# Filler matmuls of the identity in the opening, activation-table loads issued on their own, and a last sum taken bank by bank, in a windowed attention with a feed-forward layer

## The chip, the cores and the metric

The kernel runs on one core of a Trainium2 chip. The metric is the device time of one execution in microseconds (us). Before the change it is 925.33 us, the median of three runs (924.84 to 925.38).

The core has five engines with queues of their own, each strictly in the order of the program: TensorE (PE; its weight loads are shown as PEld), VectorE (DVE), ScalarE (ACT), GpSimd (POOL) and SyncE (SP), which here only issues DMAs. An instruction that waits for a semaphore holds up everything behind it on its engine.

## The reference, cut to what matters

```python
q, k, v = ...                      # 8 batches x 8 heads x 576 positions x 64, float32
scores = q @ k.T / sqrt(64)        # causal, window of 64 positions, rest masked
attn   = softmax(scores); o = attn @ v
x = o.transpose(0, 2, 1, 3).reshape(4608, 512)
h = x @ w_in                       # 512 -> 2048, weights are float64
g = h * tanh(softplus(h))          # "mish"
out = g @ w_out                    # 2048 -> 512, float32
```

## The kernel before, in words

The 4608 tokens are cut into 12 chunks of 384. The 512 channels are four pairs of heads; a *unit* is one pair of one chunk, so there are 48 units. For a unit, PE makes the scores (24 small matmuls, L322), DVE adds the mask and takes the row minimum (L343), ACT takes the exponential (L347), DVE divides by the sum (L353, L354, L356), the result is turned (in chunks 0 to 2 by PE, L377, with a copy by ACT or DVE, L382; later by a DVE transpose and 12 small DMAs, L394 and L400), and PE multiplies with v (L413). ACT and DVE split the result into a rounded part `xh` (L426) and a rest `xl` (L427).

The feed-forward layer walks over 16 slices `f` of the 2048 inner columns. `ffn_in` makes `h` for one chunk and slice with 12 matmuls of 384 columns (L439: four channel blocks, each as three products of high and low parts); `activate` applies mish on ACT (L468); `halves` splits it into two parts (`g`, on ACT and DVE in chunks 0 and 1, L476 and L477, on POOL later, L480 and L482); `ffn_out` adds 9 matmuls of 512 columns (L502) into three banks of PSUM, one for each 128 tokens: `acc0` to `acc2` (list `A`) for every chunk but chunk 1, which uses `at0` to `at2` (list `B`). After slice 15, DVE copies banks 0 and 2 and ACT bank 1 into SBUF (L515), and SP stores each (L517). The two banks `h0` and `h1` (list `H`) hold `h` in turn; only 384 of their 512 columns are used.

The weights come as 64-bit floats, one slice after the other (`st`, 1 MB each, L238), and `weights` rebuilds them as two rounded 32-bit parts: an absolute value (on ACT for slices 0 to 6, L247; on DVE afterwards, L250), four further passes on DVE (L252, L253, L255, L260), a cast on ACT (L267) and a subtraction on DVE (L270). The load of slice f waits until the L260 pass of slice f-2 is done (`pace`). This work, and the attention of chunks 0 and 1, fill the opening.

Nothing is issued in the order in which the Python code names it. Every piece of work is a `Task` with an engine, a cost from the table `COST`, a rank, and the tasks that it depends on. `Plan.order` plays the program through with these costs, engine by engine, takes at each point the ready task of the lowest rank, and the tasks are then emitted by their planned start. So a changed cost or rule moves instructions on all engines. From chunk 2 on, the PE tasks are chained in a fixed order and only the other engines are planned. ACT needs one table of functions for the exponential (and the absolute value) and another one for mish; before the change the table load is put in by the build in front of the first activation that needs it.

Of the kernel before, what the change touches and what calls it, by code (L numbers as in the profile page):

```python
# [16 lines left out]
P = 128  # L17
# [8 lines left out]
    "h": 2.08, "hcc": 0.52, "acc": 2.06, "acc1": 0.687, "scores": 0.95, "values": 0.95, "tr": 0.65,  # L26
    "ttr": 0.21, "small": 0.19, "norm3": 0.46, "norm6": 0.87, "xl": 0.47, "pT": 0.45, "turn": 0.97,
    "exp": 0.385, "xh": 0.42, "mish": 0.40, "gh": 0.46, "gl": 0.47, "poolgh": 0.51, "poolgl": 1.01,
    "abs": 1.06, "absv": 0.62, "ts": 0.62, "stt": 1.14, "wh": 0.96, "store": 0.65, "issue": 0.45, "move": 0.62,
}  # L30
LATENCY = {"PE": 0.30, "DVE": 0.16, "ACT": 0.22, "POOL": 0.16}
SELF = {"PE": 0.0, "DVE": 0.11, "ACT": 0.10, "POOL": 0.10}
TABLE_LOAD = 1.3
SLOW_UNTIL, SLOW = 70.0, 1.2
LANDING = 1.9
BYTES_PER_US = 330e3
# [19 lines left out]
class Task:  # L56
    def __init__(self, n, engine, cost, emit, rank, table, size):
        self.n, self.engine, self.cost, self.emit, self.rank = n, engine, cost, emit, rank
        self.table, self.size = table, size
        self.name = f"{cost} {rank:g}"  # L60
        self.deps, self.users = set(), []
        self.start = self.done = None


class Plan:
# [6 lines left out]
    def add(self, engine, cost, emit, reads=(), writes=(), rank=0.0, after=(), table=None, size=0, chain=False):  # L72
        t = Task(len(self.tasks), engine, COST.get(cost, cost), emit, rank, table, size)
        t.deps.update(after)
        for b in reads:
            b.read(t)
        for b in writes:
            b.write(t)
        t.deps.discard(t)
        if chain:  # L80
            if self.last_pe:
                t.deps.add(self.last_pe)
            self.last_pe = t
        self.tasks.append(t)
        return t

    def order(self):
        left = {}
        ready = {e: [] for e in ("PE", "DVE", "ACT", "POOL", "SP")}
        free = dict.fromkeys(ready, 0.0)  # L90
        free.update(SP=0.7, ACT=2.5, POOL=4.0)
        table, moving = "exp", 0.0
        for t in self.tasks:
            left[t] = len(t.deps)
            for d in t.deps:
                d.users.append(t)

        def release(t):
            return max([d.done if d.engine != t.engine or d.engine == "SP" else d.start + d.cost + SELF[d.engine]
                        for d in t.deps], default=0.0)  # L100

        for t in self.tasks:
            if not left[t]:
                ready[t.engine].append((release(t), t))
        for _ in self.tasks:
            at, e = min((max(free[e], min(r for r, _ in ready[e])), e) for e in ready if ready[e])

            def key(rt):
                r, t = rt
                switch = t.table not in (None, table)  # L110
                return t.rank + SWITCH * switch, t.n

            now = [rt for rt in ready[e] if rt[0] <= at + 1e-6]
            pick = min(now, key=key)
            ready[e].remove(pick)
            t = pick[1]
            t.start = at
            if e == "ACT" and t.table not in (None, table):
                table = t.table
                t.start += TABLE_LOAD  # L120
            free[e] = t.start + t.cost * (SLOW if e == "PE" and at < SLOW_UNTIL else 1.0)
            if e == "SP":
                moving = max(moving, t.start + LANDING) + t.size / BYTES_PER_US
                t.done = moving
            else:
                t.done = free[e] + LATENCY[e]
            for u in t.users:
                left[u] -= 1
                if not left[u]:
                    ready[u.engine].append((release(u), u))  # L130
        return sorted(self.tasks, key=lambda t: (t.start, t.n))
# [6 lines left out]
def tile_window_attn_mish_ffn(  # L138
# [229 lines left out]
    def turn_pe(u, rank, engines, chain):  # L368
        pr, prb = u.pr
        pr = pr.rearrange("p (j k) -> p j k", k=P)  # L370
        pT, pTb = u.pT = pT_ring.take()
        for h in range(2):
            t_ps, tb = u.t[h]

            def tr(h=h, t_ps=t_ps):
                for m in range(NM):
                    nc.tensor.transpose(t_ps[:, m * P:(m + 1) * P], pr[:, h * NM + m, :], ident)  # L377

            add("PE", "tr", tr, reads=[prb], writes=[tb], after=[u.normed[h]], rank=rank, chain=chain)

            def copy(h=h, t_ps=t_ps):
                (nc.scalar.copy if engines[h] == "ACT" else nc.vector.tensor_copy)(  # L382
                    pT[:, :, h * NM:(h + 1) * NM, :].rearrange("p r m i -> p m r i"),
                    t_ps[:, :CH].rearrange("p (m r i) -> p m r i", m=NM, i=32))
# [109 lines left out]
    def ffn_out(c, f, rank, chain):  # L494
        acc = B if c == 1 else A
        g, gb = pend.pop((c, f))

        def emit(banks):
            for t in banks:
                ts_ = slice(t * P, (t + 1) * P)  # L500
                for i, (a, part) in enumerate(((0, 0), (0, 1), (1, 0))):
                    nc.tensor.matmul(acc[t][0], g[:, a, ts_], ws[f][:, 1, part, :],  # L502
                                     start=f == 0 and i == 0, stop=f == NF - 1 and i == 2)

        parts = [[t] for t in range(NTT)] if f in (0, NF - 1) else [range(NTT)]
        for part in parts:
            sums[c] = add("PE", "acc" if len(part) > 1 else "acc1", lambda part=part: emit(part), reads=[gb, wbufs[f]],
                          writes=[acc[t][1] for t in part], rank=rank, chain=chain, after=[sums[c]] if c in sums else [])
        outs.append((c, f))
        pump()  # L510
        if f == NF - 1:
            for t in range(NTT):
                o, ob = o_ring.take()
                eng = "DVE" if t % 2 == 0 else "ACT"
                add(eng, "store", lambda t=t, o=o: (nc.vector.tensor_copy if t % 2 == 0 else nc.scalar.copy)(o, acc[t][0]),  # L515
                    reads=[acc[t][1]], writes=[ob], rank=-1)
                add("SP", "issue", lambda t=t, o=o: nc.sync.dma_start(out[c * CH + t * P:c * CH + (t + 1) * P, :], o),  # L517
                    reads=[ob], rank=10 ** 6, size=P * DO * 4)

    units = []  # L520
    for c in range(NCHUNK):
# [39 lines left out]
    def bank(pool):  # L561
        rot[0] += 1
        return pool[(rot[0] - 1) % 3]

    def tail(i):
        u, r = units[i], RANK_U[i]
        if i >= 4:
            pool = B if i < 8 else A
            u.t = [bank(pool), bank(pool)]
            u.o = bank(pool)  # L570
        turn_pe(u, r, ("ACT", "ACT") if 4 <= i < 8 else ("ACT", "DVE"), False)
        values(u, r, False)
        refill_v(i)
        x_parts(u, r)
# [32 lines left out]
    def late(c, f):  # L607
        ffn_out(c, f, r_ffn(c, f) + 15, False)
        if (c, f) == (0, NF - 1):
            for i in range(8, 12):  # L610
                front(i)
                if i > 8:
                    tail(i - 1)
            tail(11)
# [27 lines left out]
    for i in range(4 * NPAIR, len(units)):  # L642
        g = first + (i - 4 * NPAIR) // 2 * 2
        run(g - 2 if i >= 4 * NPAIR + 2 else (5, 6)[i % 2], "s", i)
        run(g, "v", i)
    pr_ring.extend([wa_ring.tiles[1].bitcast(F32)[:, :HM * P]], wa_ring.bufs[1:])
    step, held = 0, []
    for g, steps in enumerate(groups):
        r = 1000 + 10 * step
# [20 lines left out]
        for c, f in held:  # L670
            ffn_out(c, f, r + 15, True)
        held = steps
    for c, f in held:
        ffn_out(c, f, 10 ** 5, True)

    tasks = plan.order()
    if REPORT:
        REPORT(tasks)
    for t in tasks:
        t.emit()  # L680


# [36 lines left out]
```

## Time and profile before

| | |
|---|---|
| median of three runs | 925.33 us (924.84 to 925.38) |
| profiled execution, its own time | 925.7 us |
| its span, first to last instruction | 923.8 us |
| PE busy | 900.7 us (97%) |
| DVE, ACT, POOL busy | 315.6, 364.2, 261.3 us |
| mean granted TensorE clock | 0.993 |
| ACT table loads | 64 |

One execution is taken apart. The page of the profile gives the busy time of each engine, the groups of instructions and the chain of work that ended last. The other views are cut by time: the chain in order of time, the timeline of single instructions, the waits (who stood idle until whom), and the stretches (busy time, granted clock and DMA traffic between two points). Times in them are from the start of the span. The granted clock is 1.00 at full speed; where the clock has no record yet, at the very start, it also reads 1.00.

### The profile page before, as it was taken

What the parts mean: (1) busy time and instruction counts of PE and PEld (TensorE: products, weight loads), DVE (VectorE), ACT (ScalarE), POOL (GpSimd) and SP (SyncE); (2) the same over time, 40 slices, a digit from 0 to 9 for tenths busy, and PEclk for the clock granted to TensorE, in tenths of its full rate; (3) what the DMA queues carried; (4) which work ended last, traced back from release to release, by engine and by line L of the source; (5) the groups of instructions that cost most, each with busy time, mean ns of one, the idle gap of its engine ahead of it and who ended that gap; (6) DMA issues with size and microseconds to landing.
All of it is one profiled execution on the core that took longest, in us unless ns stands there. A gap on an engine that the chain in (4) does not pass through costs nothing.

```text
span 923.8 us, 17003 instructions
## 1 busy us (share of the span) xinstructions
PE 900.7 (97%) x6408; PEld 805.6 (87%) x6408; DVE 315.6 (34%) x969; ACT 364.2 (39%) x963; POOL 261.3 (28%) x337
## 2 busy tenths in 40 slices
PE   5779999999999999999999999999999999999998
PEld 4569998888898998899899989988998899899896
DVE  6979973442314404304124034042141240400000
ACT  6875436964634414315225134243242341411110
POOL 1000000023233323433343244233333532432432
PEclk9989999999999999999999999999999999999999
DMA  8754412222324203302312222132122220100000
GB/s 271 234 194 153 167 69 72 73 93 74 100 61 128 83 20 94 111 26 89 115 27 83 67 81 78 56 93 77 60 87 66 79 81 23 54 37 1 35 1 35
DMA packets 79763, 77.28 MB, mean 84 GB/s; under 512 B 10049, under 2 KB 73025, under 8 KB 77633
## 3 DMA queue, kind: packets, MB, share of 16 engines
q1 hardware_dynamic: 79536, 75.96, 26.0%
q8 instruction: 51, 0.84, 0.4%
q14 instruction: 32, 0.25, 0.1%
q10 hardware_dynamic: 144, 0.23, 0.1%
HBM read 56.10 MB, written 9.44 MB: 71 GB/s over the span
## 4 chain that ended last, share of the span: by engine, by line
PE 92%; DVE 4%; ACT 2%; DMA 1%; issue 0%; SPq 0%; ACTq 0%; DVEq 0%
PE h L439 43%; PE acc L502 38%; PE at L502 3%; PE at L322 3%; PE at L413 2%; PE h L413 1%; DVE pr L343 1%; DMA st<-w 1%; DVE pr L356 1%; DMA k_t<-kT 1%; PE acc L322 1%; DVE wa L255 1%; DVE wa L260 0%; ACT L468 0%; PE h L322 0%; PE acc L413 0%
## 5 line engine op out<-in xcount | busy, mean ns | idle before, releaser
L439 PE MATMUL h<-xh,w 128*128 128x384 f32 x1536 | 407.6, 338 | 3.4 <-ACT t L468 2.2
L439 PEld LDWEIGHTS h<-xh,w 128*128 128x128 f32 x1536 | 280.5, 189 | 10.6 <-ACT t L468 6.4
L502 PE MATMUL acc<-w,g 128*128 128x512 f32 x1224 | 288.0, 390 | 0.0
L502 PEld LDWEIGHTS acc<-w,g 128*128 128x128 f32 x1224 | 229.2, 188 | 48.0 <-POOL gx L482 0.3
L439 PE MATMUL h<-xl,w 128*128 128x384 f32 x768 | 258.3, 336 | 0.0
L468 ACT ACTIVATE t<-h 128x384 f32<-128x384 f32 x192 | 94.3, 492 | 395.0 <-PE h L439 394.6
L480 POOL TENSOR_SCALAR gx<-t 128x384 fp32r<-128x384 f32 x40 | 20.5, 512 | 569.4 <-ACT t L468 217.2
L439 PEld LDWEIGHTS h<-xl,w 128*128 128x128 f32 x768 | 145.0, 189 | 2.2
L482 POOL TENSOR_TENSOR g<-t,g 128x384 fp32r<-128x384 f32 x120 | 130.3, 1086 | 9.8
L343 DVE CUSTOM_DVE_ANT_0 pr<-at,mask 128x128 f32<-128x128 f32 x150 | 34.7, 286 | 251.5 <-PE at L322 251.5
L502 PE MATMUL acc<-w,gx 128*128 128x512 f32 x360 | 91.4, 398 | 0.0
L347 ACT ACTIVATE pr<-pr,mx 128x128 f32<-128x128 f32 x216 | 84.0, 391 | 8.0 <-DVE mx L343 7.8
L480 POOL TENSOR_SCALAR g<-t 128x384 fp32r<-128x384 f32 x120 | 66.5, 554 | 68.3 <-PE acc L502 42.5
L502 PEld LDWEIGHTS acc<-w,gx 128*128 128x128 f32 x360 | 65.8, 188 | 15.2 <-issue 2.8
L468 ACT ACT_TABLE_LOAD x32 | 41.1, 1283 | 60.8 <-PE h L439 60.5
L343 DVE CUSTOM_DVE_ANT_0 wa<-at,mask 128x128 f32<-128x128 f32 x57 | 13.3, 286 | 122.7 <-PE at L322 122.7
L515 DVE COPY o<-acc 128x512 f32<-128x512 f32 x22 | 14.8, 671 | 96.6 <-PE acc L502 96.6
L356 DVE TENSOR_TENSOR pr<-pr,sm 128x768 f32<-128x768 f32 (+1 forms) x40 | 42.5, 1062 | 1.0
L482 POOL TENSOR_TENSOR gx<-t,gx 128x384 fp32r<-128x384 f32 x40 | 40.5, 1012 | 3.3
L347 ACT ACTIVATION_READ_ACCUMULATOR pr<-pr,mx 128x1 f32 x216 | 40.6, 188 | 0.0
L322 PE MATMUL at<-k_t,q_t 64*64 64x128 f32 x828 | 35.2, 288 | 1.2 <-DMA k_t<-kT 1.2
L347 ACT ACT_TABLE_LOAD x28 | 35.9, 1283 | 0.5
(69 smaller groups left out, 606.3 us busy)
## 6 DMA issues: line engine op xcount, KB each, us to landing
v_t<-vN SPq DMA_DIRECT2D x48, 384.0 KB, 4.3
st<-w SPq DMA_DIRECT2D x16, 1024.0 KB, 4.8
k_t<-kT SPq DMA_DIRECT2D x47, 224.0 KB, 4.6
q_t<-qT SPq DMA_DIRECT2D x48, 192.0 KB, 4.5
out<-o SPq DMA_DIRECT2D x36, 256.0 KB, 2.3
pT<-pr SPq DMA_DIRECT2D x288, 24.0 KB, 1.8
pT<-wa SPq DMA_DIRECT2D x144, 24.0 KB, 1.8
k_t<-kT ACTq DMA_DIRECT2D x1, 224.0 KB, 3.6
```

Source lines behind the costliest of these rows:

```text
L255: x = add("DVE", "stt", lambda: nc.vector.scalar_tensor_tensor(a, words[1], 0xC0000000, a, ALU.bitwise_and, ALU.bitwise_or), after=[x], ra ...
L322: nc.tensor.matmul(t[par * BLK:(par + 1) * BLK, col:col + P], u.q[0][rows, n * BLK:(n + 1) * BLK], u.k[0][rows, n * BLK:n * BLK + P], star ...
L343: x = add("DVE", "ttr", lambda: nc.vector.tensor_tensor_reduce(out=pr[:, j, :], in0=t_s[:, col:col + P], in1=mk, op0=ALU.add, op1=ALU.min, ...
L347: return add("ACT", "exp", lambda: nc.scalar.activation(pr[:, j, :], pr[:, j, :], AF.Exp, bias=mx[:, j:j + 1], scale=-1.0, accum_out=sm[:, ...
L356: return add("DVE", "norm3" if n == NM else "norm6", lambda: nc.vector.tensor_tensor(pr[:, js, :], pr[:, js, :], sm[:, js].unsqueeze(2).to ...
L413: mm = nc.tensor.matmul(o_ps[rows, n * BLK:(n + 1) * BLK], v_t[:, n, rows], pT[:, 2 * par:2 * par + 2, h * NM + m, :], start=True, stop=True)
L439: nc.tensor.matmul(h_ps[:, :CH], ws[f][:, 0, part, cc * P:(cc + 1) * P], xx[:, cc, :], start=cc == 0 and i == 0, stop=cc == NPAIR - 1 and ...
L468: add("ACT", "mish", lambda: nc.scalar.activation(t, h_ps[:, :CH], AF.Mish), reads=[hb], writes=[tb], rank=post, table="mish")
L480: x = add("POOL", "poolgh", lambda: nc.gpsimd.tensor_scalar(g[:, 0, :], t, 1.0, 0.0, ALU.mult, ALU.add), reads=[tb], writes=[gb], rank=post)
L482: add("POOL", "poolgl", lambda: nc.gpsimd.tensor_tensor(g[:, 1, :], t, g[:, 0, :].bitcast(F32), ALU.subtract), reads=[tb], writes=[gb], af ...
L502: nc.tensor.matmul(acc[t][0], g[:, a, ts_], ws[f][:, 1, part, :], start=f == 0 and i == 0, stop=f == NF - 1 and i == 2)
L515: add(eng, "store", lambda t=t, o=o: (nc.vector.tensor_copy if t % 2 == 0 else nc.scalar.copy)(o, acc[t][0]), reads=[acc[t][1]], writes=[o ...
```

## The change: what it does

Four edits are made. Lines in this section are those of the diff or of the changed kernel.

**Fillers.** When a PE task is emitted whose planned start lies between 5 and 75 us, and the plan has PE idle before it, the loop over the tasks first emits matmuls of the identity by itself (128 by 128, 64 columns, float32) into columns 384 to 448 of bank `h0`, which nothing reads: as many as fill three quarters of the planned idle time at a cost of 0.11 us each. There are 68 of them, in 13 places: 9, 9, 5, 1, 6, 6, 2, 2, 1, 6, 4, 12 and 5.

**Table loads.** The plan lets a table load start as soon as ACT is free, and the load is now emitted as an instruction of its own, without a wait, in front of the activation. There are 58 loads where there were 64; before, 27 of the 64 carried a wait.

**The end.** The last two slices of the last chunk (14 and 15) are no longer summed slice by slice but bank by bank (`finish`). In the last bank the last slice covers 384 columns only; its last 128 columns are summed apart in bank `at0`, and DVE adds them to a copy of the 128 columns of the bank. That piece is stored by itself.

**A third buffer, earlier.** The softmax buffer that lies in the second weight buffer is handed over when the attention of chunk 2 begins (units 8 to 11), not after it.

```diff
-    "abs": 1.06, ..., "move": 0.62,
+    "abs": 1.06, ..., "move": 0.62, "warm": 0.11,
+TABLES = {"exp": "exp_and_others", "mish": "mish"}
+WARM = 5.0, 75.0
...
             if e == "ACT" and t.table not in (None, table):
-                table = t.table
-                t.start += TABLE_LOAD
+                table = t.load = t.table
+                t.start = max(at, free[e] + TABLE_LOAD)
+            t.idle = t.start - free[e]
...
+    def emit_acc(bank, c, f, g, t, lo=0, hi=DO, alone=False):
+        for i, (a, n) in enumerate(((0, 0), (0, 1), (1, 0))):
+            nc.tensor.matmul(bank[:, lo:hi], g[:, a, t * P:(t + 1) * P], ws[f][:, 1, n, lo:hi],
+                             start=(alone or f == 0) and i == 0, stop=(alone or f == NF - 1) and i == 2)
...
+    def finish(steps, rank):
+        gs = [(c, f, *pend.pop((c, f))) for c, f in steps]
+        c = gs[0][0]
+        cut = DO - P
+        for t in range(NTT):
+            o, ob = o_ring.take()
+            end = t == NTT - 1
+            reads = [gb for _, _, _, gb in gs] + [wbufs[f] for _, f, _, _ in gs]
+            def emit(t=t, end=end):
+                for c, f, g, _ in gs:
+                    whole = not (end and f == NF - 1)
+                    emit_acc(A[t][0], c, f, g, t, 0, DO if whole else cut)
+            add("PE", 1.37, emit, reads=reads, writes=[A[t][1]], rank=rank, chain=True)
+            if end:
+                _, f, g, _ = gs[-1]
+                add("PE", 0.2, lambda: emit_acc(B[0][0], c, f, g, t, cut, DO, True), reads=reads, writes=[B[0][1]], rank=rank, chain=True)
+                evacuate("ACT", o, ob, A[t], 0, cut)
+                store(c, t, o, ob, 0, cut)
+                o2, ob2 = o_ring.take()
+                x = evacuate("DVE", o2, ob2, A[t], cut, DO)
+                add("DVE", 0.2, lambda: nc.vector.tensor_tensor(o2[:, cut:], B[0][0][:, cut:], o2[:, cut:], ALU.add),
+                    reads=[B[0][1]], writes=[ob2], after=[x], rank=-1)
+                store(c, t, o2, ob2, cut, DO)
+            else:
+                evacuate("DVE" if t % 2 == 0 else "ACT", o, ob, A[t], 0, DO)
+                store(c, t, o, ob, 0, DO)
...
     def late(c, f):
         ffn_out(c, f, r_ffn(c, f) + 15, False)
         if (c, f) == (0, NF - 1):
+            pr_ring.extend([wa_ring.tiles[1].bitcast(F32)[:, :HM * P]], wa_ring.bufs[1:])
...
-    for c, f in held:
+    for c, f in held[:-2]:
         ffn_out(c, f, 10 ** 5, True)
+    finish(held[-2:], 10 ** 5)
...
     for t in tasks:
+        if t.load:
+            nc.scalar.preload_act_table_set(TABLES[t.load])
+        if t.engine == "PE" and WARM[0] < t.start < WARM[1]:
+            for _ in range(int(0.75 * t.idle / COST["warm"])):
+                nc.tensor.matmul(H[0][0][:, CH:CH + BLK], ident, ident[:, :BLK], start=True, stop=True)
         t.emit()
```

Three places on PE show what the emission makes of it. A semaphore in brackets is what the row waits for (`DMAHW` a DMA, `Activation_49` ACT, `DVE_49` DVE, `Pool_49` POOL).

The first place is the queue of PE after the scores of the first unit (banks `acc`), ahead of those of the second (banks `at`). Before:

```order
L322 MATMUL acc_121<-k_t_91,q_t_89 64x128
L322 MATMUL acc_122<-k_t_91,q_t_89 64x128
L322 MATMUL at_124<-k_t_92,q_t_90 64x128 [waits DMAHW4_49,DMAHW3_49]
L322 MATMUL at_125<-k_t_92,q_t_90 64x128
L322 MATMUL at_124<-k_t_92,q_t_90 64x128
```

And now:

```order
L325 MATMUL acc_121<-k_t_91,q_t_89 64x128
L325 MATMUL acc_122<-k_t_91,q_t_89 64x128
L728 MATMUL h_127<-ident 128x64 [waits Pool_49]
L728 MATMUL h_127<-ident 128x64 x8
L325 MATMUL at_124<-k_t_92,q_t_90 64x128 [waits DMAHW4_49,DMAHW3_49]
```

Nine fillers stand ahead of the second unit's scores; their only wait is for the identity that POOL makes.

The second place is the queue of PE about 60 us into the span: the end of an `ffn_out` of chunk 0, and the `ffn_in` that writes bank `h0` (`h_127`) next. Before:

```order
L502 MATMUL acc_121<-w,g_110 128x512 [waits DVE_49]
L502 MATMUL acc_122<-w,g_110 128x512 x3
L502 MATMUL acc_123<-w,g_110 128x512 x3
L439 MATMUL h_127<-xh_117,w 128x384 [waits Activation_49]
L439 MATMUL h_127<-xl_118,w 128x384
```

And now:

```order
L516 MATMUL acc_121<-w,g_110 128x512 [waits DVE_49]
L516 MATMUL acc_122<-w,g_110 128x512 x3
L516 MATMUL acc_123<-w,g_110 128x512 x3
L728 MATMUL h_127<-ident 128x64 [waits Activation_49]
L728 MATMUL h_127<-ident 128x64 x4
L442 MATMUL h_127<-xh_117,w 128x384
```

Five fillers stand between, and the wait for ACT, which the first matmul of `h` had, is now on the first of them: they write the same bank, and that bank is free when ACT has read it.

The third place is the end of PE's queue. Before:

```order
L502 MATMUL acc_121<-w,g_109 128x512 x3
L502 MATMUL acc_122<-w,g_109 128x512 x3
L502 MATMUL acc_123<-w,g_109 128x512 x3
L502 MATMUL acc_121<-w,g_110 128x512 x3
L502 MATMUL acc_122<-w,g_110 128x512 x3
L502 MATMUL acc_123<-w,g_110 128x512 x3
```

And now:

```order
L516 MATMUL acc_121<-w,g_109 128x512 x3
L516 MATMUL acc_121<-w,g_110 128x512 x3
L516 MATMUL acc_122<-w,g_109 128x512 x3
L516 MATMUL acc_122<-w,g_110 128x512 x3
L516 MATMUL acc_123<-w,g_109 128x512 x3
L516 MATMUL acc_123<-w,g_110 128x384 x3
L516 MATMUL at_124<-w,g_110 128x128 x3
```

The first bank is complete after 6 matmuls of the 18 where it was after 12, the second after 12 where it was after 15, and three matmuls of 128 columns are added at the end.

In between, from the chunk-0 sums to about 200 us, the plan also moves the attention of units 8 to 11 and some casts and weight passes against each other on PE, ACT and DVE; the number of matmuls there is the same.

More of the change, by code (lines that the diff above doesn't have):

```diff
@@ L28 @@
     "exp": 0.385, "xh": 0.42, "mish": 0.40, "gh": 0.46, "gl": 0.47, "poolgh": 0.51, "poolgl": 1.01,
-    "abs": 1.06, "absv": 0.62, "ts": 0.62, "stt": 1.14, "wh": 0.96, "store": 0.65, "issue": 0.45, "move": 0.62,
+    "abs": 1.06, "absv": 0.62, "ts": 0.62, "stt": 1.14, "wh": 0.96, "store": 0.65, "issue": 0.45, "move": 0.62, "warm": 0.11,
 }
@@ L61, in __init__ @@
         self.deps, self.users = set(), []
-        self.start = self.done = None
+        self.start = self.done = self.load = None
 class Plan:
@@ L496, in ffn_out @@
         g, gb = pend.pop((c, f))
[L498 to L503, printed above, removed]
         parts = [[t] for t in range(NTT)] if f in (0, NF - 1) else [range(NTT)]
         for part in parts:
-            sums[c] = add("PE", "acc" if len(part) > 1 else "acc1", lambda part=part: emit(part), reads=[gb, wbufs[f]],
-                          writes=[acc[t][1] for t in part], rank=rank, chain=chain, after=[sums[c]] if c in sums else [])
+            sums[c] = add("PE", "acc" if len(part) > 1 else "acc1", lambda part=part: [emit_acc(acc[t][0], c, f, g, t) for t in part],
+                          reads=[gb, wbufs[f]], writes=[acc[t][1] for t in part], rank=rank, chain=chain,
+                          after=[sums[c]] if c in sums else [])
         outs.append((c, f))
@@ L513, in ffn_out @@
                 o, ob = o_ring.take()
[L514 to L518, printed above, removed]
+                evacuate("DVE" if t % 2 == 0 else "ACT", o, ob, acc[t], 0, DO)
@@ new lines, in ffn_out, with evacuate @@
+                store(c, t, o, ob, 0, DO)
[3 more added lines that the diff above has]
+                             start=(alone or f == 0) and i == 0, stop=(alone or f == NF - 1) and i == 2)
+    def evacuate(eng, o, ob, bank, lo, hi):
+        copy = nc.vector.tensor_copy if eng == "DVE" else nc.scalar.copy
+        return add(eng, 0.15 + (hi - lo) / 1024, lambda: copy(o[:, lo:hi], bank[0][:, lo:hi]), reads=[bank[1]], writes=[ob], rank=-1)
@@ new lines, in store @@
+    def store(c, t, o, ob, lo, hi):
+        add("SP", "issue", lambda: nc.sync.dma_start(out[c * CH + t * P:c * CH + (t + 1) * P, lo:hi], o[:, lo:hi]),
+            reads=[ob], rank=10 ** 6, size=P * (hi - lo) * 4)
+    def finish(steps, rank):
[23 more added lines that the diff above has]
+                evacuate("DVE" if t % 2 == 0 else "ACT", o, ob, A[t], 0, DO)
+                store(c, t, o, ob, 0, DO)
@@ L563, in bank @@
         return pool[(rot[0] - 1) % 3]
+    BY_DMA = ()
     def tail(i):
         u, r = units[i], RANK_U[i]
+        if i in BY_DMA:
+            turn_dma(u, r)
+        else:
+            if i >= 4:
+                pool = B if i < 8 else A
+                u.t = [bank(pool), bank(pool)]
+            turn_pe(u, r, ("ACT", "ACT") if 4 <= i < 8 else ("ACT", "DVE"), False)
         if i >= 4:
[L568 to L571, printed above, removed]
+            u.o = bank(B if i < 8 else A)
         values(u, r, False)
@@ L645, in tile_window_attn_mish_ffn @@
         run(g, "v", i)
-    pr_ring.extend([wa_ring.tiles[1].bitcast(F32)[:, :HM * P]], wa_ring.bufs[1:])
     step, held = 0, []
```

## The prediction

> **What bounds the kernel now.** I read the busy times of long stretches first, then the chain of waits in order of time, then stretches of one clock period. The columns are the busy time of PE, PEld, DVE, ACT and POOL, the granted clock, the DMA share and the traffic.
>
> ```profile
> core 0: us, PE busy (x) PEld busy (x) DVE busy (x) ACT busy (x) POOL busy (x), PEclk, DMA share, GB/s
> 0.00:73.00 73.00, 53.88 (x541) 43.22 (x541) 58.52 (x181) 55.90 (x148) 4.22 (x17) 0.91 0.70 228
> 73.00:920.00 847.00, 846.82 (x5868) 762.40 (x5868) 256.39 (x789) 308.31 (x816) 257.08 (x320) 1.00 0.23 71
> ```
>
> From 73 to 920 us PE is busy for 846.8 of 847.0 us at full clock. The change leaves the matmuls there as they are, so only two stretches can move the time by more than a few tenths: the opening (19.1 us of PE idle) and what follows the last matmul.
>
> In the opening the chain (start, duration, what) leaves PE:
>
> ```profile
> 48.99 1.11 DVE wa L260
> 50.11 7.07 DMA st<-w
> 57.27 1.12 ACT wa L247
> 58.77 1.28 ACT L468
> 60.07 0.50 ACT t L468
> 60.61 6.03 PE h L439 x24
> 72.94 4.43 PE h L439 x24
> 81.50 4.18 PE h L439 x24
> ```
>
> A weight pass on DVE allows the next weight load; the load takes 7.07 us; ACT takes its absolute value, loads the mish table, does mish, and only then may PE write bank `h0`. So DVE's work up to 50.1 us, then the load, then ACT set the start of PE's gapless stream at 60.61. For DVE, the waits of the opening (total, times, longest):
>
> ```profile
> DVE pr L343 <- PE acc L322: 6.2, 1, 6.2
> DVE wa L252 <- ACT wa L247: 2.8, 2, 1.8
> DVE pT L382 <- PE h L377: 1.0, 1, 1.0
> DVE pr L343 <- PE at L322: 0.6, 1, 0.6
> ```
>
> A faster PE can give DVE back only the last two rows, 1.6 us, beside the first scores.
>
> The last rows needed are those of the clock. Its changes lie on a grid of 3.41 us:
>
> ```profile
> 6.16:9.57 3.41, 1.56 (x24) 1.19 (x24) 2.48 (x19) 2.87 (x15) 0.00 (x0) 1.00 1.12 286
> 16.40:19.81 3.41, 1.52 (x26) 1.17 (x27) 3.34 (x14) 3.11 (x11) 0.00 (x0) 1.00 1.04 324
> 19.81:23.22 3.41, 3.02 (x35) 2.33 (x39) 3.38 (x15) 2.61 (x12) 0.00 (x0) 0.50 0.41 119
> 33.46:36.88 3.42, 1.71 (x39) 1.40 (x35) 3.39 (x10) 2.56 (x4) 0.00 (x0) 1.00 0.72 213
> 57.36:60.77 3.41, 1.25 (x6) 0.72 (x5) 2.39 (x5) 3.35 (x5) 0.00 (x0) 1.00 0.38 114
> 60.77:64.18 3.41, 3.41 (x12) 3.41 (x13) 3.38 (x5) 1.38 (x2) 0.00 (x0) 0.50 0.32 72
> ```
>
> After a stretch with 1.25 or 1.52 us of PE work the next one is granted 0.50; after 1.71 it stays at 1.00. Only the half-clock stretch from 60.77 is on the chain: its 24 matmuls took 6.03 us, against 4.18 at full clock (81.50), so it costs 1.85.
>
> The Trainium skill, "TensorE: Matmul & The Clock Gate", Part 1, says that the clock is decided in windows of 3413 ns that run on freely, whatever the program does. The grid agrees with the length.
>
> **The fillers.** No row shows a 64-column matmul of the identity. The nearest rows are these:
>
> ```profile
> 4.47 1.56 PE L322 MATMUL acc<-k_t,q_t 64*64 64x128 f32 x24 [4.47 <-DMA k_t<-kT]
> 7.19 1.56 PE L322 MATMUL at<-k_t,q_t 64*64 64x128 f32 x24 [1.16 <-DMA k_t<-kT]
> 15.25 0.89 PE L322 MATMUL at<-k_t,q_t 64*64 64x128 f32 x24
> 32.89 0.91 PE L413 MATMUL at<-pT,v_t 128*64 128x64 f32 x22 [0.25 <-ACT pT L382]
> 30.30 0.94 PE L377 MATMUL at<-ident,pr 128*128 128x128 f32 x6 [0.56 <-DVE pr L356]
> 51.01 1.54 PE L377 MATMUL at<-ident,pr 128*128 128x128 f32 x6 [2.83 <-DVE pr L356]
> ```
>
> The products with v also have 64 columns, but change weights seldom: 0.91/22 = 0.04 us each. The transposes load 128 by 128 weights each time, as a filler may, with twice the columns: 0.94/6 = 0.16 at full clock, 1.54/6 = 0.26 at half. I take 0.08 and 0.16, between these; the ends stay in the range.
>
> Early on: scores of one kind take 1.56 us at 4.47 and 7.19 and 0.89 at 15.25, so PE is slow until about 13 us whatever PEclk reads there. The stretch 6.16 to 9.57 holds 1.56 us of PE work; nine slow fillers add 1.44, which passes 1.71, so PE should be fast from 9.57. The scores and transposes up to 13 us then save about 1.0. Against it: the nine stand ahead of the second unit's scores, which waited only 1.16 for their load, so 1.44 - 1.16 = 0.3 is delay (1.2 at 0.26 each). And much of the gain ends at a load:
>
> ```profile
> 13.38 1.16 ACT L247 ACTIVATE wa<-st 128x1024 f32<-128x1024 f32 x1 [0.79 <-DMA st<-w]
> 24.78 0.28 DVE L343 CUSTOM_DVE_ANT_0 pr<-at,mask 128x128 f32<-128x128 f32 x1
> 60.61 0.57 PE L439 MATMUL h<-xh,w 128*128 128x384 f32 x1 [2.16 <-ACT t L468]
> ```
>
> ACT's pass at 13.38 waits 0.79 for its data, and DVE waits for that pass. I take -0.3 for the start of DVE's work (-0.7 to +0.8). The other fillers up to 53 us fill idle time of PE and move no one who is late; the tightest place is six fillers shortly before the scores at 22.91 (1.56 long, done 24.47, read at 24.78): 0.3 of slack.
>
> The last five fillers are different. They write `h0`, so they wait for the same mish as the real `h`, and stand in front of it. They fill nothing of the gap of 2.16 us up to 60.61; they cost 5 x 0.08 = 0.4. And they can't raise the clock: the gap lies within 57.36:60.77, its length stays, and with it the 1.25 us of work. So the start of PE's stream moves by -0.3 + 0.4 = +0.1. If PE started early, the cover of the DVE passes would go and the load be late next; it is already.
>
> **The table loads.**
>
> ```profile
> 58.77 1.28 ACT L468 ACT_TABLE_LOAD   x1
> 57.27 1.12 ACT L247 ACTIVATE wa<-st 128x1024 f32<-128x1024 f32 x1 [1.32 <-DMA st<-w]
> L468 ACT ACT_TABLE_LOAD x32 | 41.1, 1283 | 60.8 <-PE h L439 60.5
> ```
>
> In the opening the load at 58.77 did not wait for data: ACT was busy from 57.27 up to it. Dropping the wait gives 0 there. Later, loads did wait (60.5 us in all for `h`), but PE never ran short of mish, which hides them: 0. Six loads fewer are 6 x 1.28 = 7.7 us of ACT, beside PE: 0. If the moved attention of units 8 to 11 ate its slack, a wait of up to 0.5 could appear; I take 0.
>
> The Trainium skill, "ScalarE: Activation LUTs", section "What ACT_TABLE_LOAD costs", counts about 1380 ns of draining beside the 1283 ns. Here the activation began at 60.07, 0.02 us after the load ended, so the trace doesn't show it; by the page six loads would be 16 us, off the path all the same.
>
> **The end.** The chain, the timeline, and DMA rows (GB/s in 40 slices of 915 to 924 us; KB each and us to landing):
>
> ```profile
> 903.60 16.38 PE acc L502 x72
> 919.32 0.59 ACT L515 COPY o<-acc 128x512 f32<-128x512 f32 x1 [15.11 <-PE acc L502]
> 920.00 0.69 DVE L515 COPY o<-acc 128x512 f32<-128x512 f32 x1 [0.67 <-PE acc L502]
> GB/s 0 0 0 0 0 0 0 0 0 0 0 0 0 0 0 0 0 0 0 0 0 0 0 337 382 382 392 382 355 392 373 400 100 0 0 0 0 0 0 0
> out<-o SPq DMA_DIRECT2D x3, 256.0 KB, 2.0
> pT<-pr SPq DMA_DIRECT2D x288, 24.0 KB, 1.8
> ```
>
> Now: last matmul at 919.97, copy to 920.69, last issue about 920.72, landing about 2.0 later, 922.7, and about 1.1 to the end of the span at 923.8. After: a matmul of 512 columns is 16.38/72 = 0.23, of 384 4.18/24 = 0.17, so each 128 columns are about 0.06. The 384-column part ends 0.2 earlier, 919.8, the three short ones at about 920.0. ACT copies 384 columns (about 0.49, from 0.59 for 512) to 920.33. DVE's copy reads the same bank and I let it come behind ACT's: about 0.25 to 920.6, the addition 0.28 (as the 128-column pass at 24.78) to 920.9. The last issue is then 0.25 *later*, 920.97. But it carries 64 KB, not 256, and the banks before it have left by then: it lands after 1.5 (2.0 less the 0.5 that the missing 192 KB take at 380 GB/s) to 1.8 (the row of 24 KB): 922.5 to 922.8. I take -0.2; if copies don't wait for each other -0.6, if the added steps take longer +0.3.
>
> **Sum.** 925.7 (the profiled execution) + 0.1 + 0 - 0.2 = 925.6; it lies 0.37 above the median of the runs, so 925.2. What a measurement here can tell from no change is 0.2%, 1.85 us: 923.5 to 927.2 counts as the same.
>
> **Rivals.** *Faster: the load at 50 us is not late.* The load took 7.07 us; the median of its kind is 4.8:
>
> ```profile
> st<-w SPq DMA_DIRECT2D x16, 1024.0 KB, 4.8
> ```
>
> Landed by 54.9, ACT would go on at 55.95 (57.27 less the 1.32 that it waited): 925.2 - 1.3 = 923.9. A gap of 0.84 leaves 2.6 us of work in the stretch, so the clock holds too: another 1.85, 922.0. Middle 922.9. For it: all queues shift a little, and one load of 16 was this slow. Against: nothing takes traffic away from it. It decides when the work in the stretch before `h` passes 1.7. Chance 0.2.
>
> *Faster: the clock's grid lies elsewhere.* A boundary that cuts the gap of 2.16 with under 1.70 (3.41 - 1.71) on either side leaves both stretches busy enough; that is 1.24 of 3.41, 0.36 of all positions. 925.2 - 1.85 = 923.35 (and the stretch at 50 us lies off the path). Against: three runs lie within 0.54 us of each other, so the grid seems tied to the program. Chance 0.13. This is what the free-running window of the Trainium skill's page on TensorE and its clock gate, Part 1, would bring.
>
> *Slower: fillers ahead of ready work.* At the transposes' 0.26 the nine before the second scores delay them by 1.2 and the six near 22 us by 1.3 (1.56 - 0.3); DVE, busy 3.34 to 3.39 of 3.41 in the rows of the clock, passes on at least 1.0 of this, the last five cost 1.3 instead of 0.4: 925.2 + 0.3 + 1.0 + 0.5 to 0.9, about 927.1 (926.0 to 928.0). It decides from 1.16/9 = 0.13 us for one filler. Chance 0.14.
>
> *The change doesn't do what it says*: that the fillers keep the clock up before `h` is what I expect not to happen; this is my forecast, chance 0.53.
>
> **How the numbers follow.** Forecast 925.2 (924.3 to 926.3). The range goes down into the first rival to 922.3, leaving about 0.1 out, and up to 926.9. Faster by over 0.2%: most of the two faster rivals, 0.27; slower: just under half of the second and a little of mine, 0.08; the same 0.65.
>
> **What would show it.** Right: fillers near 60 us directly ahead of `h` behind one mish, granted 0.50 behind them, h x24 near 6.0; scores at 0.89 soon after 10 us; last issue near 921.0, landing near 922.5. Wrong: a weight load landing near 5 us after its issue at 50, or a granted 1.00 at the start of the stream; fillers over 0.13 each; idle time of PE beyond 73 us.

## The result, and the profile after

The changed kernel takes 930.96 us (median; the six runs lie from 930.10 to 933.32), the kernel before 925.36 in the same comparison. The ratio is 1.0065, with a 95% interval of 1.0053 to 1.0077: slower by about 6 us, where 925.2 was forecast with a range of 922.3 to 926.9. The profiled execution took 930.38 us, its span 928.6. Two executions of later comparisons, of 1481.55 us (the kernel before) and 5034.55 us (the table loads alone), are left out of all ratios and spreads below.

First the long stretches of the changed kernel, with the columns of the prediction:

```profile
0.00:73.00 73.00, 61.77 (x644) 53.16 (x645) 54.92 (x176) 49.87 (x140) 4.25 (x17) 0.98 0.67 214
73.00:920.00 847.00, 846.72 (x5882) 764.81 (x5881) 259.55 (x791) 306.15 (x816) 257.90 (x320) 1.00 0.23 72
```

PE is again busy from 73 us on. In the opening it is *busier* than before (61.8 us of 73, 53.9 before) and its granted clock reads higher (0.98, 0.91 before), and still everything is later. Both numbers mislead: more of PE's work is fillers, and the clock reads 1.00 up to 18 us although the scores there take their half-clock time, as the next view shows. The chain of waits in order of time, from the start to the gapless stream of PE:

```profile
4.49 1.56 PE acc L325 x24
6.05 4.03 PE h L728 x18
10.08 1.49 PE at L325 x24
11.57 4.03 PE h L728 x18
15.60 0.64 PE h L380 x3
16.24 1.49 PE acc L325 x24
...
54.43 1.11 DVE wa L263
55.56 7.37 DMA st<-w
63.02 1.12 ACT wa L250
64.14 0.37 ACT xh L429
64.52 1.28 ACT L725
65.82 0.50 ACT t L471
66.36 2.01 PE h L728 x10
68.37 5.17 PE h L442 x24
```

The fillers (L728) are on the chain itself. Nine of them stand in the trace as 18 matmuls: PE runs each of these float32 products as two. They take 4.03 us, 0.22 each, so one filler costs 0.45 us at half clock. The scores of the third unit still take 1.49 at 16.24, the half-clock duration; the first scores at 0.89 come at 21.50 in this trace, though PE had no gap from 4.49 up to there. The start of the last weight pass before the late load moved from 48.99 to 54.43, by 5.44 us; the load itself took 7.37 (7.07 before); the five fillers before `h` took 2.01; and `h` started at 68.37 where it was 60.61.

That is 7.76 us late, but the whole is only 4.8 us longer: from the start of `h` to the end of the span the changed kernel takes 860.2 us, the kernel before 863.2. Two things were given back. The 24 matmuls of `h` took 5.17 for 6.03 (0.86), since the fillers had used up part of the half-clock stretch. The other 2.1 us can't be seen in PE's row; what shows them is the waits of PEld, the engine row that holds the weight loads; first of the kernel before, then of the changed kernel, both from 75 us on (total, times, longest):

```profile
PEld h L439 <- ACT t L468: 3.3, 17, 0.5
```

```profile
PEld h L442 <- ACT t L471: 1.3, 4, 0.5
```

Seventeen waits of weight loads for mish have become four, 2.0 us of waiting less, in the stretch in which PE was busy for 846.8 of 847.0 us. The end, last:

```profile
924.33 0.48 PEld L516 LDWEIGHTS at<-w,g 128*128 128x128 f32 x3
924.50 0.44 PE L516 MATMUL at<-w,g 128*128 128x128 f32 x3
924.70 0.48 ACT L521 COPY o<-acc 128x384 f32<-128x384 f32 x1 [0.61 <-PE acc L516]
925.22 0.29 DVE L521 COPY o<-acc 128x128 f32<-128x128 f32 x1 [2.38 <-ACT o L521]
925.61 0.29 DVE L550 TENSOR_TENSOR o<-at,o 128x128 f32<-128x128 f32 x1
out<-o SPq DMA_DIRECT2D x1, 64.0 KB, 1.6
```

DVE's copy waits for ACT's, as forecast, and the small store lands after 1.6 us. From the last matmul (924.94) to the end of the span (928.56) it is 3.6 us; before, from 919.97 to 923.83, it was 3.9.

### The profile page after: what moved, and what is told of

It is laid out like the page before. It is cut to its first block, busy times and chain, and to the rows that moved or that the text cites. A ratio compares the mean times of both kernels' runs of the same rounds, so it can differ in the third digit from the quotient of the medians.

```text
span 928.6 us, 17277 instructions
## 1 busy us (share of the span) xinstructions
PE 913.4 (98%) x6547; PEld 822.1 (89%) x6547; DVE 315.8 (34%) x970; ACT 357.1 (38%) x958; POOL 262.1 (28%) x337
## 4 chain that ended last, share of the span: by engine, by line
PE 92%; DVE 4%; ACT 2%; DMA 1%; issue 0%; ACTq 0%; DVEq 0%
PE h L442 42%; PE acc L516 38%; PE at L516 3%; PE at L325 3%; PE at L416 2%; PE h L416 1%; PE h L728 1%; DMA st<-w 1%; DVE pr L346 1%; ACT L725 1%; PE acc L325 1%; DVE pr L359 1%; DVE wa L258 1%; ACT pr L350 0%; DVE wa L263 0%; PE h L325 0%
## 5 line engine op out<-in xcount | busy, mean ns | idle before, releaser
L350 ACT ACTIVATE pr<-pr,mx 128x128 f32<-128x128 f32 x204 | 79.3, 390 | 11.9 <-DVE mx L346 11.5
L521 DVE COPY o<-acc 128x512 f32<-128x512 f32 (+1 forms) x22 | 14.4, 654 | 97.0 <-PE acc L516 94.6
L359 DVE TENSOR_TENSOR pr<-pr,sm 128x768 f32<-128x768 f32 (+1 forms) x38 | 40.6, 1068 | 0.9
L350 ACT ACTIVATION_READ_ACCUMULATOR pr<-pr,mx 128x1 f32 x204 | 38.3, 188 | 0.0
L516 PE MATMUL at<-w,g 128*128 128x512 f32 (+1 forms) x147 | 35.7, 392 | 0.0
```

The source lines that it names most:

```text
L350: return add("ACT", "exp", lambda: nc.scalar.activation(pr[:, j, :], pr[:, j, :], AF.Exp, bias=mx[:, j:j + 1], scale=-1.0, accum_out=sm[:, ...
L359: return add("DVE", "norm3" if n == NM else "norm6", lambda: nc.vector.tensor_tensor(pr[:, js, :], pr[:, js, :], sm[:, js].unsqueeze(2).to ...
L516: nc.tensor.matmul(bank[:, lo:hi], g[:, a, t * P:(t + 1) * P], ws[f][:, 1, n, lo:hi], start=(alone or f == 0) and i == 0, stop=(alone or f ...
L521: return add(eng, 0.15 + (hi - lo) / 1024, lambda: copy(o[:, lo:hi], bank[0][:, lo:hi]), reads=[bank[1]], writes=[ob], rank=-1)
```

## The experiments

Ratios are to the kernel before, run on the same chip in the same comparison, with 95% intervals; 0.1% is 0.93 us. A difference between two of these ratios is uncertain by 1.1 to 1.9 us.

**Without fillers.**

```diff
-WARM = 5.0, 75.0
+WARM = 0.0, 0.0
```

> All 68 fillers are taken out, the other three edits stay. Theory P (price): a filler is two PE instructions of 0.22 us each at half clock, and the two places of nine before 16 us push all of DVE's opening work back by 5.4 us. Then nearly the whole loss goes: 925.0 (924.4 to 925.8), with DVE's pass that releases the late weight load near 49 us again. Theory M (moved work): the loss comes from the moved attention and the table loads without a wait; then it stays at 929 to 931.

Measured: 922.29 us, 0.9963 (0.9951 to 0.9976), faster than both theories. Theory M falls. The fillers cost about 1% and the rest of the change *gains* a third of one, which neither the prediction nor this expectation had. In the profile the weight load landed in time this time:

```profile
55.74 2.22 ACT L250 ACTIVATE wa<-st 128x1024 f32<-128x1024 f32 x2
58.35 1.28 ACT L725 ACT_TABLE_LOAD   x1
```

Two passes on ACT without a wait between them, where the kernel before waits 1.32 us.

**Without the first two places, and without the last.** A counter of the places sets the count to zero; the second kernel has (13,) for (1, 2).

```diff
+            if place in (1, 2):
+                n = 0
```

> Only the first two places (nine fillers each, 6.0 to 10.1 and 11.5 to 15.6 us in the changed kernel) are left without fillers. Theory P: the opening comes back by 5.4 us, the other fillers stay, the five before h still cost about 2.0 less 0.9 of clock: 926.0 (925.2 to 926.8), with PE at full clock near 13 us. Theory M: 929 to 931. A third way, that each place costs in proportion to its fillers (18 of 68): 929.4.

Measured: 927.18, 1.0020 (1.0003 to 1.0036). Of the 1.0065, 0.45% or 4.2 us are gone: the first two places are the largest part, and with 4.2 (2.3 to 6.1) no more than the 5.4 that Theory P took from one trace. In the profile of this kernel DVE's pass before the late load starts at 51.78, 2.65 us earlier than in the changed kernel and not 5.44: the other fillers delay it too.

> Only the last place (five fillers before h at 66.4 us) is left without fillers. Theory P: 2.0 us go, but h then starts earlier in the half-clock stretch and its 24 matmuls take 6.0 again instead of 5.2: 929.8 (929.2 to 930.4). Rival: those five hold up h by their whole 2.0 us and the clock has nothing to do with it: 929.0.

Measured: 929.30, 1.0036 (1.0024 to 1.0048): by the ratios 2.7 us less than the changed kernel, uncertain by 1.6 us. In the profile `h` takes 6.04 from 66.81, so the clock does give back part of what is saved. Which of the two sizes is right, 1.1 or 2.0, these intervals can't tell.

**Fillers of 128 columns.**

```diff
-                nc.tensor.matmul(H[0][0][:, CH:CH + BLK], ident, ident[:, :BLK], start=True, stop=True)
+                nc.tensor.matmul(H[0][0][:, CH:CH + P], ident, ident, start=True, stop=True)
```

> The same 68 fillers, with 128 columns for 64. If the load of 128 by 128 weights sets their price, 18 of them still take about 4.0 us at half clock, and the time differs from the changed kernel only through the clock: if the clock answers to the columns that stream, PE is at full clock near 12 to 15.6 us, not 19, and the time is 929.0 (928 to 930). If the columns set the price, the first two places take 6 to 8 us each and the time is 935 to 939. If neither matters, 930.9 as before.

Measured: 925.83, 1.0004 (0.9992 to 1.0016): twice the columns, and 0.6% *faster* than the changed kernel, faster than any of the three expectations had it, though still 0.4% slower than without fillers. The timeline of PE and PEld shows why; of this kernel:

```profile
6.07 3.87 PE L728 MATMUL h<-ident 128*128 128x128 f32 x18
6.07 3.68 PEld L728 LDWEIGHTS h<-ident 128*128 128x128 f32 x18 [0.33 <-issue]
9.87 0.89 PE L325 MATMUL at<-k_t,q_t 64*64 64x128 f32 x24
10.69 2.27 PE L728 MATMUL h<-ident 128*128 128x128 f32 x18
12.80 0.49 PE L380 MATMUL h<-ident,pr 128*128 128x128 f32 x3
```

And of the changed kernel:

```profile
5.98 4.10 PE L728 MATMUL h<-ident 128*128 128x64 f32 x18
5.98 3.91 PEld L728 LDWEIGHTS h<-ident 128*128 128x128 f32 x18 [0.33 <-issue]
10.01 1.56 PE L325 MATMUL at<-k_t,q_t 64*64 64x128 f32 x24
11.50 4.10 PE L728 MATMUL h<-ident 128*128 128x64 f32 x18
15.39 0.85 PE L380 MATMUL h<-ident,pr 128*128 128x128 f32 x3
```

The first nine cost about the same with either width (3.87 and 4.10), so the columns don't set the price; what both have in common is a weight load with each matmul, and the weight loads fill nearly all of that time (3.68 and 3.91). But behind the wide ones the scores take 0.89 at 9.87 and the next nine take 2.27, behind the narrow ones 1.56 at 10.01 and the next nine again 4.10. That is not the chance of one trace: in all four traces with narrow fillers in the first two places (the changed kernel's, the one without the last place, and the two with the last place in the other bank) the third unit's scores at 16.1 to 16.2 still take 1.56, and the first scores at 0.89 come at 21.50 to 23.49. The wide ones were traced once, but the 5 us between the two kernels are those of twelve and six executions. So the columns make the difference, and the busy time of PE's row isn't what the clock answers to. What exactly it counts is not shown. Narrow fillers made PE look busy here and left it slow.

**The table loads alone.** From the kernel without fillers; the third buffer is handed over where it was before, and the end is the old one:

```diff
-    for c, f in held[:-2]:
+    for c, f in held:
         ffn_out(c, f, 10 ** 5, True)
-    finish(held[-2:], 10 ** 5)
```

> The kernel before with the edit of the table loads alone (the plan's rule and the load issued without a wait); no fillers, the end and the third buffer as before. Theory L: the 2.9 us that the three other edits gain come mostly from here: in the kernel before, the load of the mish table waits for h once in every two chunks, mish ends 0.05 us before the next matmuls of that bank, and the weight load of those waits 0.18 us: 14 times about 0.13 us, 1.85 us, beside up to 0.8 in the opening: 923.0 (922.4 to 923.8) against 925.2. Theory O (the opening): the gain comes from a weight load that lands in time, which depends on the whole plan: then 924.3 to 925.5.

Measured: 924.20, 0.9977 (0.9966 to 0.9989). A second run, for the waits of PEld:

> The edit of the table loads alone once more, since the profile of the first time is of an execution that can't be compared. Expected 0.9977 of before again (0.996 to 0.999), with PE's weight loads waiting for mish 3 times or so after 75 us, where they do 17 times before.

Measured: 923.62, 0.9965 (0.9951 to 0.9979). Theory L, at its size: with the loads alone nearly all of the gain of the kernel without fillers (0.9963) is there. The waits of PEld from 75 us on:

```profile
PEld h L442 <- ACT t L471: 0.8, 3, 0.5
```

**The end alone.** From the kernel without fillers; the third buffer as before, and the loads too:

```diff
-                table = t.load = t.table
-                t.start = max(at, free[e] + TABLE_LOAD)
+                table = t.table
+                t.start += TABLE_LOAD
...
-        if t.load:
-            nc.scalar.preload_act_table_set(TABLES[t.load])
```

> The kernel before with the new end alone. From the changed kernel's trace: its last matmul to the end of the span takes 3.6 us where it took 3.9 before, and three matmuls of 128 columns cost 0.2 to 0.4: -0.1 (-0.5 to +0.4), 925.1 against 925.2. A rival that puts the other gain here: 923.5 or less.

Measured: 925.21, 0.9998 (0.9987 to 1.0009): -0.1 us was expected, and nothing can be seen. The third buffer was never run by itself: the kernel without fillers (0.9963, later 0.9969) and the loads alone (0.9977, 0.9965) leave for it and the end together less than the intervals.

**The plan kept, the loads put back behind a wait.** From the kernel without fillers:

```diff
-        if t.load:
-            nc.scalar.preload_act_table_set(TABLES[t.load])
```

> The kernel without fillers (922.3) with its plan kept as it is, but with the table loads put in by the build again, so that a load waits for what its activation waits for. Theory L: the 0.13 us stalls return, 14 times or so, and up to 1.28 us in the opening where a load has to wait: 924.2 (923.8 to 925.5). Theory O: the plan is the same and so is the time, 922.3 (within 0.6).

Measured: 925.68, 0.9997 (0.9987 to 1.0006): the whole gain is gone, 0.34% or 3.1 us, with the plan of the work and the 58 loads kept. So it is the wait on the load. The rows of PEld read 3.3, 17, 0.5 again. Two traces say where: this one, and one of the kernel without fillers (its second run, below), both with `h` at 6.01 behind a late load. Their rows of `h` on the chain, in this order:

```profile
62.35 6.01 PE h L442 x24
```

```profile
60.26 6.01 PE h L442 x24
```

To the ends of their spans (925.4 and 921.3) it is 863.0 and 861.0 us: 2.0 us are lost from `h` on, with 2.5 us more of these waits. The other 2.1 us between these two traces lie in the opening.

One of these places in the kernel before, on ACT and on the two rows of PE:

```profile
322.31 1.28 ACT L468 ACT_TABLE_LOAD   x1 [4.28 <-PE h L439]
323.60 0.49 ACT L468 ACTIVATE t<-h 128x384 f32<-128x384 f32 x1
323.95 0.64 PE L439 MATMUL h<-xh,w 128*128 128x384 f32 x2
324.15 0.19 PEld L439 LDWEIGHTS h<-xh,w 128*128 128x128 f32 x1 [0.18 <-ACT t L468]
324.25 0.19 PEld L439 LDWEIGHTS h<-xl,w 128*128 128x128 f32 x1
324.43 0.34 PE L439 MATMUL h<-xl,w 128*128 128x384 f32 x1
```

And the same place in the changed kernel, on ACT:

```profile
325.15 1.28 ACT L725 ACT_TABLE_LOAD   x1
329.43 0.49 ACT L471 ACTIVATE t<-h 128x384 f32<-128x384 f32 x1 [3.00 <-PE h L442]
331.51 0.49 ACT L471 ACTIVATE t<-h 128x384 f32<-128x384 f32 x1 [1.59 <-PE h L442]
```

Before, ACT stood idle for 4.28 us, loaded the table only when `h` was there (1.28), and finished mish at 324.09, when PE had reached the matmul that writes the same bank. Its weights were held up 0.18. The matmuls follow each other at 0.17, but from the one at 324.15 to the next at 324.43 it is 0.28. PE's row shows no idle time, because the ends of matmuls in it are modelled and overlap the next. After, ACT has loaded the table at 325.15, right behind its work before, and has then only `h` to wait for.

**The last place in the other bank**, `h1`, which ACT had read earlier, with nine fillers for five:

```diff
-            for _ in range(int(0.75 * t.idle / COST["warm"])):
-                nc.tensor.matmul(H[0][0][:, CH:CH + BLK], ident, ident[:, :BLK], start=True, stop=True)
+            last = place == 13 and n > 0
+            for _ in range(9 if last else n):
+                nc.tensor.matmul(H[last][0][:, CH:CH + BLK], ident, ident[:, :BLK], start=True, stop=True)
```

> The changed kernel with the fillers of the last place written to bank h1, which ACT has already read, nine of them for five; all others stay. If the five cost what they cost because they wait for the same mish as h, these nine run inside the gap of 3.2 us (9 x 0.23 = 2.1), h starts 2.0 us earlier, at 66.4, and if 64-column fillers hold the clock, its 24 matmuls take 4.2: 930.9 - 2.0 - 1.0 = 927.9 (927.2 to 928.5). If they fill the gap but don't hold the clock, 6.0 us: 929.5, as without them. If the bank is not the point, no change: 930.9.

Measured: 928.79, 1.0032 (1.0020 to 1.0044). The fillers now run in the gap (64.67 to 66.79 in the profile) and `h` starts right behind mish; the bank was the point. But in this trace the clock fell all the same, and `h` took 5.78. The trace is of the slowest of the nine executions. Such a half-clock stretch of 3.41 us takes 0.0018 off the mean granted clock of an execution (half of 3.41/929); the mean is 0.998 in the traced one, and 0.999 or 1.000 in six of the nine, so in these six the clock did not fall again after the opening. With 128 columns in that last place:

> As the kernel with nine fillers of the last place in bank h1, but these nine with 128 columns (the other places keep 64). With 64 columns they filled 2.1 us of the gap and the clock fell all the same, h took 5.8. If the clock answers to columns, the wide ones hold it and h takes 4.2 to 4.6: 1.2 us under that kernel, 927.6. If any idle time of 1.6 us in that stretch makes it fall, h stays at 5.8 and the time at 928.8.

Measured: 927.89, 1.0012 (1.0001 to 1.0023), by the ratios 0.2% or 1.9 us under it, uncertain by 1.5 us. The stretch with the fillers and the next one, first with 64 columns, then with 128:

```profile
64.49:67.91 3.42, 2.30 (x20) 2.12 (x18) 1.76 (x4) 2.88 (x4) 0.00 (x0) 1.00 0.24 69
67.91:71.32 3.41, 2.96 (x9) 2.96 (x10) 3.38 (x6) 1.96 (x3) 0.00 (x0) 0.50 0.22 31
```

```profile
64.24:67.65 3.41, 2.67 (x21) 2.40 (x21) 2.52 (x5) 3.35 (x5) 0.00 (x0) 1.00 0.25 74
67.65:71.06 3.41, 3.41 (x21) 3.41 (x21) 3.38 (x5) 1.82 (x3) 0.00 (x0) 1.00 0.43 108
```

In these traces narrow fillers with 2.30 us of busy time didn't hold the clock, where 1.71 us of ordinary work did in the kernel before, and the wide ones held it, with 2.67. The pair doesn't separate the columns from the rest: in the second trace the load landed sooner (6.92 us for 7.71), and PE stood idle before `h` for 0.74 us and not 1.57. Over all executions, the wide ones have a mean clock of 0.999 or 1.000 in twelve of twelve, the narrow ones in six of nine, and the median of those six, 927.96, is nearly that of the wide ones. That 128 columns hold the clock better in this place is likely, but not shown.

**Without fillers again.**

> The kernel without fillers once more. In its profile the weight load issued at 51 us landed in time (before 55.7), in those of before and of five variants it took 7 to 7.8 us. If that was this kernel's order of transfers, it lands in time again and the time is 0.9963 of before (0.995 to 0.9975). If it was chance, the load takes about 7 us again in this profile, h starts near 61 us, and the time lies in the same range only by the 14 stalls that are gone (0.9975 to 0.9985).

Measured: 924.17, 0.9969 (0.9957 to 0.9980), the same as the first time within the intervals; but the load took 7.04 us here, in the fastest of the nine executions, and the half-clock stretch lay on `h`:

```profile
57.35:60.76 3.41, 1.44 (x8) 0.94 (x7) 2.69 (x4) 3.34 (x5) 0.00 (x0) 1.00 0.35 104
60.76:64.17 3.41, 3.41 (x12) 3.41 (x11) 3.38 (x5) 1.13 (x2) 0.00 (x0) 0.50 0.40 127
```

In the first profile of the same kernel it lay before it, and `h`, from 60.18, ran at full clock:

```profile
52.88:56.29 3.41, 3.19 (x10) 2.72 (x9) 2.24 (x3) 3.38 (x6) 0.00 (x0) 0.50 0.70 283
59.70:63.12 3.42, 3.16 (x18) 2.94 (x18) 3.38 (x6) 2.36 (x4) 0.00 (x0) 1.00 0.49 92
```

The load landed in time in the trace of the loads alone too. So the load in time was chance, and so is where the clock's stretches fall: both change from one execution to the next. The expectation tied the ratio to the load and was wrong in that: late load and 0.9969 came together.

**Wide matmuls at the very start**, of zeros and without the fillers, while PE waits for its first data:

```diff
     tasks = plan.order()
+    zero = t_ring.tiles[3][:, :P]
+    nc.vector.memset(zero, 0.0)
+    for _ in range(8):
+        nc.tensor.matmul(H[0][0][:, CH:CH + P], zero, zero, start=True, stop=True)
```

> The kernel without fillers, with eight matmuls of 128 columns on a tile of zeros put at the very start, where PE waits for the first loads until 4.5 us (8 x 2 x 0.215 = 3.4 us, from about 1.1). If columns that stream raise the clock, PE is at full clock by 4.8 to 8.2 us instead of 13 to 15, the scores of units 1 to 3 take 0.9 for 1.56, and DVE's work starts up to 1.0 us earlier, less what the load at 13.4 holds back: 0.3 to 0.8 us under the kernel without fillers. If the place was the fault of the fillers and not the columns, no more than 0.2 is seen either way. If fillers cost in any place, slower by 1 or more.

Measured: 923.23, 0.9960 (0.9944 to 0.9976), not to be told from 0.9969 in the same comparison. The second unit's scores did take 0.89, at 6.99, but the clock fell again:

```profile
6.86:10.27 3.41, 1.64 (x39) 1.29 (x43) 3.07 (x23) 3.41 (x18) 0.00 (x0) 1.00 0.87 241
10.27:13.69 3.42, 3.42 (x47) 2.53 (x38) 2.92 (x17) 1.77 (x9) 0.00 (x0) 0.50 1.02 333
```

The faster PE did its work of that stretch in 1.64 us and waited, and the next stretch was granted half. Where PE is idle they cost nothing that could be measured, and they bring nothing either.

**The middle places alone, the first place alone.**

> The changed kernel with fillers only in the ten places between (3 to 12). By difference from the runs so far they cost 8.7 - 3.8 - 1.7 = 3.2 us over the kernel without fillers. If costs add up, 0.3% above that kernel, about the time of before (ratio 0.999 to 1.002). If the first two places cost more than their own time because they also keep the clock down for all behind them, the middle ones alone cost less, about 1 us (ratio 0.997 to 0.999).

Measured: 924.80, 0.9986 (0.9976 to 0.9996), 0.20% or 1.9 us over the kernel without fillers (0.9966, the mean of its two ratios). The ratio lies in the range of the second expectation (0.997 to 0.999), and its interval reaches into that of the first: this run doesn't decide between them.

> The changed kernel with fillers only in the first place (nine, ahead of the second unit's scores). By price alone 4.03 us less the 1.1 that PE would have waited there: 2.9 us over the kernel without fillers (ratio 0.9997 to 1.0010). If DVE's later waits take most of it up, 1 us or less (ratio 0.9965 to 0.9985). If the clock also comes up later by a step of 3.4 us, 4 us or more (ratio over 1.001).

Measured: 925.27, 0.9997 (0.9989 to 1.0006), 0.31% or 2.9 us over it: the price of the nine by themselves, 4.03 less the 1.1 that PE would have waited. Its trace agrees: `h` starts at 63.50, 3.2 us behind the 60.26 of the kernel without fillers, with a late load and 6.01 us for `h` in both. By the times the costs about add up: 4.2 for the first two places, 1.9 for the ten between, 2.7 for the last make 8.8, and the fillers together cost 0.99%, 9.2 us. With 1.2 to 1.9 us of uncertainty on each this is a loose test; the second place was never run by itself, and the trace without the first two places says that their delay and that of the places between overlap.

## Why the prediction was wrong, point by point

**Fillers, the failed step: the price of one.** The prediction took 0.08 us at full and 0.16 at half clock and reached up to 0.26. The rows that it used count matmuls of the trace, and one filler is two of them, each with a weight load of its own; at half clock one takes 0.22, nearer to the transposes' 0.26 than to the 0.16 taken. Together 0.45 (4.03/9). At that price the nine before the second scores delay them by 2.9 us and not by 0.3, and the next nine stand in front of the first transposes in the same way. The trace shows the prediction's own sign of being wrong, fillers over 0.13 each. The slower rival named this mechanism, the first place and the point from which it decides (0.13 us), and was given 0.14; it too was priced too low, 927.1. The "other fillers up to 53 us", which were to "move no one who is late", were put at nothing: the ten places between cost 1.9 us (0.7 to 3.1).

**Fillers, the second failed step: that they raise the clock.** The prediction held PE's busy time against the 1.71 us at which the clock had stayed up, and gave 1.0 us of gain for a full clock from 9.57. Measured with 64 columns: half clock still at 16.24. With 128 columns: full clock at 9.87. The busy time of PE's row isn't the measure that the clock goes by; which one it is stays open.

**The five before `h`.** That they wait for the same mish and stand in front of `h` was right, and the other bank showed it; their cost was 2.01 us in the trace, not 0.4.

**Table loads, the third failed step: "PE never ran short of mish, which hides them: 0".** It came from PE's row, which had no wait from 73 us on. PEld's row had 17, for 3.3 us, and went to 3. The loads are worth 2.1 to 3.2 us (0.9977, 0.9965). With the same plan, 2.0 us of it are lost behind the start of `h` when the loads wait again (863.0 for 861.0); for the rest the opening is left, where the position of the clock's stretches and of the late load move the time by as much from one execution to the next, and it is not shown.

**The end:** -0.2 forecast, 0.9998 (0.9987 to 1.0009) measured, which can't tell -0.2 from nothing; copies and issue came in the order that was forecast.

**The clock's grid:** "the grid seems tied to the program" was wrong; three runs within 0.54 us were too few. In later comparisons, on four chips, the kernel before spread from 923.5 to 928.8. The Trainium skill, "TensorE: Matmul & The Clock Gate", Part 1, says that the window runs on freely and the warm-up differs from run to run. The two placings of the half-clock stretch in the two profiles of the kernel without fillers agree with that, and its length of 3.41 us does too. The same part of the Trainium skill also says that what is issued after some 3.4 us runs at the full clock; here the trace of the changed kernel speaks against it, with PE occupied from 4.49 and the scores at 16.24 still taking 1.49.

**Sum.** Forecast: +0.1 in the opening, 0, -0.2. Measured: fillers +9.2, the other edits together -3.1 (0.9966), 1.0065 in all.

## What to carry to other kernels

A matmul that is only to keep the clock up has a price: here that of its weight loads, about 0.25 us at full and 0.45 at half clock, with 64 or with 128 columns. The narrow ones didn't raise the clock in the first two places; the wide ones did, and the kernel with them was still 0.4% slower than the one without. If such a matmul is tried, it should stream many columns and stand where PE waits for something that it doesn't itself wait for: look at the semaphore of the bank it writes. Price an added instruction by the trace's count for one call, not by one row's mean. Before a wait is called hidden, look at the waits of the weight loads as well: PE's row can be 100% busy and still lose 0.1 us at each of them; a table load that does not need the data is best issued ahead of the wait for it, which was worth 0.34% here.

## What the runs showed of the hardware

- One float32 matmul of 128 by 128 weights and 64 or 128 columns stands as two in the trace and took 0.43 to 0.46 us at half clock (18 in 3.87 and 4.10); at full clock 0.25 (18 of 128 columns in 2.27).
- 64-column matmuls back to back from 6 to 10 and 11.5 to 15.6 us didn't bring the clock up, in four traces; 128-column ones did within 3.9 us, in the one trace with them.
- A PE at full clock can finish early and fall back: 1.64 us of work in a stretch, and the next one at 0.50.
- PE's row can read busy throughout (846.8 of 847.0 us) while its weight loads wait: 14 fewer such waits, 2.5 us in sum, were worth 2.0 us from `h` on.
